# Attention values and the next unit's scores: two runs of small matmuls, or one alternating stream

## The chip, the cores and the metric

The kernel runs on one core of one Trainium2 chip. The metric is the device time of one execution in microseconds (us); a lower time is better. The core has TensorE (PE in the profile, with its weight loads on a row of their own, PEld), VectorE (DVE), ScalarE (ACT), GpSimd (POOL) and SyncE (SP, which issues the transfers).

## The reference

Inputs are q, k and v of shape 8 x 8 x 576 x 64 (batch, heads, sequence, head dimension), and the weights of a gated feed-forward layer.

```python
rel = pos[:, None] - pos[None, :]
mask = (rel >= 0) & (rel < 64)                      # a window of 64 positions
attn = softmax(where(mask, q @ k.T / 8, -1e9))
x = (attn @ v)  # heads side by side: 8 x 576 x 512
h = relu(x @ w_in)                                  # 512 -> 1024
c = conv along the sequence, 3 taps, per channel, zero at the ends
out = (h * sigmoid(c)) @ w_out                      # 1024 -> 512
```

## The kernel before

**Units.** Batch and sequence are laid out in one line of 4608 positions and cut into NU = 12 units of NX = 384. A unit holds NT = 6 blocks of 64 positions. The 8 heads are worked on as NC = 4 groups c (or b) of two heads, so each of the two matmul kinds below comes in four calls a unit.

**Scores** (`qk(u, b)`, line 320). In units 2 to 11 a call multiplies a stationary piece of q, 64 rows (one head's 64 dimensions) by 32 columns (32 positions), with a moving piece of k of 96 positions. The result goes to PSUM partitions `p * 64 + s`, so the columns of the array that a call uses follow from p (0 or 1, the half) and s (0 or 32, the quarter within it); the head h chooses the upper or lower 64 rows of the array and the PSUM tile, `sc[0]` or `sc[1]`. One call is 24 matmuls, which go over eight 64 x 32 pieces of the array. In units 0 and 1 the pieces are 64 x 64 (`wide(u)`), and a call is 12 matmuls.

**Values** (`values(u, c)`, line 437). A call multiplies 128 x 64 stationary pieces of v, using all rows of the array and one half of its columns (head h decides which half), with 64 moving columns of the transposed weights `ub`. One call is 12 matmuls, 6 for each half, h alternating. The result goes to `acc[0]` or `acc[1]`.

All of these are of type f32, and the hardware runs an f32 matmul as two passes: the trace has 24 records for a call of `values` and 48 for a call of `qk` on 64 x 32 pieces.

**The feed-forward part** (`mm1`, line 458, and `mm2`, line 518) is 192 matmuls a unit on the whole 128 x 128 array, 384 or 386 columns each, fp32r with hi and lo parts (three products). Between these matmuls the planner puts the calls of `values` of the next unit and of `qk` of the one after it.

**Who waits for whom.** `row_max` (DVE, line 337) reads `sc` after a call of `qk`, and the next call of `qk` may only write `sc` when it is done. After a call of `values`, `split_hi` (ACT) and `split_lo` (DVE) write `xh` and `xl` of that group, which `mm1` of the unit reads.

**What sets the order.** All work is put into a list by `at(t, engine, cost, ...)`, with a wanted time t, an estimated cost and the tiles that it reads (r) and writes (w). `queued` (line 57) plays the list through with these costs and writes out the order of each engine. It charges 0.12 us when PE goes from one `kind` of matmul to another (`SWITCH`), and where the plan leaves PE idle in the first 110 us it puts in idle matmuls on the tile `spare` (`keep_busy`, line 196). The costs and the 0.12 are numbers of this planner and not measured times. The wanted times of `qk` stand right behind those of `values`, and the key `("turn", c)`, which both write, keeps the calls in turn:

```python
at(t, "PE", 0.70 if wide(u) else 0.62, lambda b=b: qk(u, b), ..., w=bank_keys(u, b) + [("turn", b)],
   kind="tiled" if wide(u) else "eight")                                       # qk, in softmax
at(t, "PE", 0.72, lambda: values(u, c), ..., w=[("acc", ("v", u, c)), ("turn", c)],
   kind="tiled")                                                               # values, in attend
```

Of the kernel before, what the change touches and what calls it, by code (L numbers as in the profile page):

```python
# [15 lines left out]
P = 128  # L16
W = 64
HW = W // 2
KW = W + HW
B, H, S, D = 8, 8, 576, 64  # L20
DM, DFF = H * D, 1024
SB = S // W
NT = 6
NX = NT * W
NU = B * S // NX
# [130 lines left out]
def attention_moe(ctx: ExitStack, tc: tile.TileContext, q, k, v, w_in, conv_w, w_out, out):  # L156
    nc = tc.nc
# [4 lines left out]
    def many(n, shape, dt, name, where=pool):  # L162
        return [where.tile(shape, dt, name=f"{name}{i}") for i in range(n)]

    NB = NT // 2
    ub = many(2, [P, 4, 2 * NT, 32], F32, "ub")
# [7 lines left out]
    qs = pool.tile([P, NC, NX], F32, name="q")  # L174
    ks = pool.tile([P, NC, NX + W], F32, name="k")
    vs = pool.tile([P, NC, NT, 2, D], F32, name="v")
# [14 lines left out]
    acc = many(2, [P, 512], F32, "acc", psum)  # L191
# [15 lines left out]
    def at(t, eng, cost, do, r=(), w=(), kind=None, mb=0):  # L207
        plan.append(Work(t, eng, cost, do, list(r), list(w), kind, mb))
# [76 lines left out]
    def wide(u):  # L285
        return u < BY_PE

    def block(u, b, i):

        first = (u * NT + b % 2 * NB + i) % SB == 0  # L290
        return (P, W if first else 0, 0) if wide(u) else (KW, 0, 2 if first else 1)
# [22 lines left out]
    def banks_of(u, b):  # L314
        return {1: po[2:], 2: po[:2]}.get(b, sc) if u == 0 else sc

    def bank_keys(u, b):
        return {1: [("po", 2), ("po", 3)], 2: [("po", 0), ("po", 1)]}.get(b, [("sc", 0)]) if u == 0 else [("sc", 0)]

    def qk(u, b):  # L320
        g, t0 = b // 2, b % 2 * NB
        rows = W if wide(u) else HW
        for i in range(NB):
            n, o, _ = block(u, b, i)
            for p in range(2):
                for s in range(0, W, rows):
                    r, t = p * W + s, (t0 + i) * W + s
                    for h in range(2):
                        hs = slice(h * D, (h + 1) * D)
                        nc.tensor.matmul(banks_of(u, b)[h][r:r + rows, i * P + o:i * P + n], qs[hs, 2 * g + p, t:t + rows],  # L330
                                         ks[hs, 2 * g + p, t + o:t + n], start=True, stop=True)

    def row_max(u, b):
        for i in range(NB):
            n, o, m = block(u, b, i)
            for h in range(2):
                nc.vector.tensor_tensor_reduce(  # L337
                    out=ss[b][:, i, h, o:n], in0=banks_of(u, b)[h][:, i * P + o:i * P + n], in1=mask[m][:, o:n],
                    scale=-0.125, scalar=3.0e38, op0=ALU.add, op1=ALU.min,
                    accum_out=nms[b][:, 2 * i + h:2 * i + h + 1])  # L340

    def exps(u, b, i):
        n, o, _ = block(u, b, i)
        for h in range(2):
            e = slice(2 * i + h, 2 * i + h + 1)
            x = ss[b][:, i, h, o:n]
            nc.scalar.activation(x, x, AF.Exp, bias=nms[b][:, e], scale=-1.0, accum_out=sms[b][:, e])  # L347

    def guard(b, on):
        on.tensor_scalar_add(sms[b], sms[b], 1e-9)  # L350

    def reciprocal(b):
        nc.vector.reciprocal(rs[b], sms[b])  # L353

    def normalise(u, b, on):
        n = P if wide(u) else KW
        sv = ss[b].rearrange("p t h k -> p (t h) k")[:, :, :n]
        on.tensor_tensor(sv, sv, rs[b].unsqueeze(2).broadcast_to([P, 2 * NB, n]), ALU.mult)  # L358
# [3 lines left out]
    def transpose_pe(b, j):  # L362
        for i in range(NB):
            nc.tensor.transpose(po[b % 2 * 2 + j][:, i * P:(i + 1) * P],
                                ss[b].rearrange("p t h k -> p (t h) k")[:, NB * j + i], ident)

    def untile(b, j):
        o = b % 2 * 2 * NB + NB * j
        nc.scalar.copy(ub[b // 2][:, :, o:o + NB, :].rearrange("p i t q -> p t i q"),  # L369
                       po[b % 2 * 2 + j][:, :NB * P].rearrange("p (t i q) -> p t i q", i=4, q=32))  # L370

    def transpose(b):
        o = b % 2 * 2 * NB
        nc.vector.transpose(
            tbuf[:, b // 2, :3, o:o + 2 * NB, :].rearrange("p j t q -> p t j q"),
            ss[b].rearrange("p t h (j q) -> p (t h) j q", q=HW)[:, :, :3])
# [6 lines left out]
    def place(g, i):  # L383
        for j in range(3):
            o = HW * (i % 2 + j)
            nc.sync.dma_start(ub[g][o:o + HW, i], tbuf[HW * i:HW * (i + 1), g, j])

    def softmax(u, qk_at, ex_at):
        for b in range(4):
            g, t = b // 2, qk_at[b]  # L390
            at(t, "PE", 0.70 if wide(u) else 0.62, lambda b=b: qk(u, b), r=[("q", g, b % 2)] + [("k", g, i) for i in range(b % 2 + 1)], w=bank_keys(u, b) + [("turn", b)],
               kind="tiled" if wide(u) else "eight")
            for i in range(NB):
                if block(u, b, i)[1]:
                    at(t + 0.1, "POOL", 0.2, lambda b=b, i=i: nc.gpsimd.memset(ss[b][:, i, :, :W], 0.0), w=[("s", b, i)])
            at(t + 0.17, "DVE", 1.27 if wide(u) else 1.1, lambda b=b: row_max(u, b),
               r=bank_keys(u, b) + (["mask0"] if wide(u) else ["mask1", "mask2"]), w=[("s", b, i) for i in range(NB)] + [("nm", b)])
            t = ex_at[b]
            for i in range(NB):
                at(t, "ACT", 0.78 if wide(u) else 0.74, lambda b=b, i=i: exps(u, b, i), r=[("nm", b)],  # L400
                   w=[("s", b, i), ("sm", b, i)], kind="exp")
            t += 0.45
            sw = [("sm", b, i) for i in range(NB)]
            if u < 3:
                at(t, "POOL", 0.6, lambda b=b: guard(b, nc.gpsimd), w=sw)
            else:
                at(t, "DVE", 0.15, lambda b=b: guard(b, nc.vector), w=sw)
            at(t, "DVE", 0.15, lambda b=b: reciprocal(b), r=sw, w=[("r", b)])
            if u < 3:
                at(t, "DVE", 1.02 if wide(u) else 0.72, lambda b=b: normalise(u, b, nc.vector), r=[("r", b)], w=[("s", b, i) for i in range(NB)])  # L410
            else:
                at(t, "POOL", 1.15, lambda b=b: normalise(u, b, nc.gpsimd), r=[("r", b)], w=[("s", b, i) for i in range(NB)])
            t += 0.4
            sr = [("s", b, i) for i in range(NB)]
            if u < BY_PE:
                for j in range(2):
                    m = ("po", b % 2 * 2 + j)
                    at(t, "PE", 0.5, lambda b=b, j=j: transpose_pe(b, j), r=sr + ["mask0"], w=[m])
                    at(t + 0.1, "ACT", 0.45, lambda b=b, j=j: untile(b, j), r=[m], w=[("u", g, i) for i in range(4)])
            else:  # L420
                t = max(t, when[-1][2] + 0.1)
                at(t, "DVE", 0.72, lambda b=b: transpose(b), r=sr, w=[("T", g)] + [("bits", i, a) for i in T_BITS[g] for a in range(2)])
                if b % 2:
                    if u == BY_PE:
                        at(t + 0.01, "POOL", 1.0, lambda g=g: zero_blocks(g), w=[("u", g, i) for i in range(4)])
                    for i in range(4):
                        at(t + 0.05, "SP", 2.1, lambda g=g, i=i: place(g, i), r=[("T", g)], w=[("u", g, i)], mb=0.15)

    banks, turn = {}, [0]

    def bank(key):
        if key not in banks:
            banks[key] = turn[0] % 2
            turn[0] += 1
        return banks[key]

    def values(u, c):
        g, p = divmod(c, 2)
        for t in range(NT):
            for h in range(2):  # L440
                nc.tensor.matmul(acc[bank(("v", u, c))][h * D:(h + 1) * D, t * W:(t + 1) * W], vs[:, c, t, h],  # L441
                                 ub[g][:, 2 * p:2 * p + 2, 2 * t + h], start=True, stop=True)

    def split_hi(u, c):
        nc.scalar.copy(xh[u % 2][:, c], acc[bank(("v", u, c))][:, :NX])
# [3 lines left out]

    def attend(u, c, t):  # L450
        g, x = c // 2, u % 2
        at(t, "PE", 0.72, lambda: values(u, c), r=[("v", g)] + [("u", g, i) for i in range(4)], w=[("acc", ("v", u, c)), ("turn", c)],
           kind="tiled")
        at(t + 0.1, "ACT", 0.4, lambda: split_hi(u, c), r=[("acc", ("v", u, c))], w=[("xh", x, c)])
        at(t + 0.2, "DVE", 0.48, lambda: split_lo(u, c), r=[("acc", ("v", u, c)), ("xh", x, c)], w=[("xl", x, c)])

# [149 lines left out]
    kind = None  # L606
    for x in plan:
        if x.eng == "ACT" and x.kind:
            (x.r if x.kind == kind else x.w).append("table")
            kind = x.kind  # L610
# [73 lines left out]
```

## Time and profile before

| | us |
|---|---|
| median of 3 runs (533.0 to 533.41) | 533.32 |
| the profiled execution, time | 533.38 |
| the profiled execution, span from first to last instruction | 531.6 |

| engine | busy us | share of the span |
|---|---|---|
| PE | 523.1 | 98% |
| PE weight loads | 499.2 | 94% |
| ACT | 405.5 | 76% |
| DVE | 381.1 | 72% |
| POOL | 115.9 | 22% |

The granted clock of TensorE is 0.998 over the span. In the rows of the profile a matmul's duration reaches past the start of the next one, since matmuls are pipelined; what a piece of work takes on PE is read from one start to the next. In the names of a row, `acc<-ub,v` is a call of `values`, `sc<-k,q` one of `qk`, `acc<-xh,wih` and the like `mm1`, `po<-gh,woh` and the like `mm2`, and `acc<-spare` an idle matmul. A form such as `64*32 64x96` means a stationary piece of 64 rows and 32 columns and a moving piece of 64 x 96.

### The profile page before, as it was taken

What the parts mean: (1) busy time and instruction counts of PE and PEld (TensorE: products, weight loads), DVE (VectorE), ACT (ScalarE), POOL (GpSimd) and SP (SyncE); (2) the same over time, 40 slices, a digit from 0 to 9 for tenths busy, and PEclk for the clock granted to TensorE, in tenths of its full rate; (3) what the DMA queues carried; (4) which work ended last, traced back from release to release, by engine and by line L of the source; (5) the groups of instructions that cost most, each with busy time, mean ns of one, the idle gap of its engine ahead of it and who ended that gap; (6) DMA issues with size and microseconds to landing.
All of it is one profiled execution on the core that took longest, in us unless ns stands there. A gap on an engine that the chain in (4) does not pass through costs nothing.

```text
span 531.6 us, 14870 instructions
## 1 busy us (share of the span) xinstructions
PE 523.1 (98%) x5802; PEld 499.2 (94%) x5802; DVE 381.1 (72%) x1108; ACT 405.5 (76%) x1034; POOL 115.9 (22%) x208
## 2 busy tenths in 40 slices
PE   9999999999999999999999999999999999999996
PEld 8888889999999999999999999999999999999996
DVE  4899999986677677676686776776776865864552
ACT  5889886799888788689689679779769769653541
POOL 6556663203121121112012022022022011100000
PEclk9999999999999999999999999999999999999999
DMA  8883760166472282273173164254155133110011
GB/s 286 318 300 123 263 224 20 27 181 211 125 249 55 76 252 65 76 236 85 48 241 106 42 222 132 47 198 156 46 185 170 46 121 105 46 61 0 1 60 61
DMA packets 29318, 69.98 MB, mean 132 GB/s; under 512 B 5696, under 2 KB 17472, under 8 KB 29248
## 3 DMA queue, kind: packets, MB, share of 16 engines
q1 hardware_dynamic: 29248, 69.03, 40.5%
q8 instruction: 46, 0.75, 0.6%
q14 instruction: 24, 0.20, 0.1%
HBM read 47.73 MB, written 9.47 MB: 108 GB/s over the span
## 4 chain that ended last, share of the span: by engine, by line
PE 88%; DVE 10%; ACT 1%; issue 1%; POOL 0%
PE po L524 38%; PE acc L461 35%; PE acc L441 6%; PE sc L330 6%; PE acc L201 2%; DVE w L241 1%; DVE c L495 1%; DVE s L337 1%; DVE w L237 1%; DVE wil L255 1%; DVE s L358 1%; DVE w L235 1%; DVE xl L448 1%; ACT ub L369 0%; ACT s L347 0%
## 5 line engine op out<-in xcount | busy, mean ns | idle before, releaser
L524 PE MATMUL po<-gh,woh 128*128 128x386 f32 (+1 forms) x384 | 133.1, 347 | 0.0
L461 PE MATMUL acc<-xh,wih 128*128 128x384 f32 x384 | 131.9, 344 | 1.1 <-DVE xl L448 0.9
L461 PE MATMUL acc<-xh,wil 128*128 128x384 f32 x384 | 129.8, 338 | 0.4 <-DVE wil L255 0.4
L524 PE MATMUL po<-gl,woh 128*128 128x386 f32 (+1 forms) x384 | 130.1, 339 | 0.0
L461 PE MATMUL acc<-xl,wih 128*128 128x384 f32 x384 | 129.7, 338 | 0.0
L524 PE MATMUL po<-gh,wol 128*128 128x386 f32 (+1 forms) x384 | 129.7, 338 | 0.0
L495 DVE SCALAR_TENSOR_TENSOR c<-hbuf,cw,c 128x386 f32<-128x386 f32 (+1 forms) x192 | 110.8, 628 | 19.9 <-ACT c L488 19.0
L347 ACT ACTIVATE s<-s,nm 128x96 f32<-128x96 f32 (+2 forms) x288 | 105.6, 371 | 9.7 <-DVE nm L337 9.3
L358 POOL TENSOR_TENSOR s<-s,r 128x576 f32<-128x576 f32 x36 | 45.7, 1271 | 196.4 <-DVE r L353 196.4
L524 PEld LDWEIGHTS po<-gh,woh 128*128 128x128 f32 x384 | 72.3, 188 | 4.3
L461 PEld LDWEIGHTS acc<-xh,wih 128*128 128x128 f32 x384 | 72.1, 188 | 4.2 <-DVE xl L448 1.6
L461 PEld LDWEIGHTS acc<-xh,wil 128*128 128x128 f32 x384 | 72.2, 188 | 0.7 <-DVE wil L255 0.7
L524 PEld LDWEIGHTS po<-gl,woh 128*128 128x128 f32 x384 | 72.4, 188 | 0.0
L524 PEld LDWEIGHTS po<-gh,wol 128*128 128x128 f32 x384 | 72.4, 188 | 0.0
L461 PEld LDWEIGHTS acc<-xl,wih 128*128 128x128 f32 x384 | 72.1, 188 | 0.0
L337 DVE CUSTOM_DVE_ANT_0 s<-sc,mask 128x96 f32<-128x96 f32 (+2 forms) x276 | 53.2, 254 | 21.3 <-PE sc L330 20.5
L515 DVE TENSOR_TENSOR gl<-c,gh 128x772 fp32r<-128x772 f32 (+1 forms) x48 | 52.8, 1099 | 20.1 <-ACT gh L511 19.5
L502 ACT ACTIVATE c<-c 128x772 f32<-128x772 f32 (+1 forms) x48 | 40.8, 850 | 33.8 <-DVE c L495 33.5
L482 ACT ACTIVATE hbuf<-acc 128x384 f32<-128x384 f32 x64 | 30.6, 487 | 34.7 <-PE acc L461 34.1
L347 ACT ACTIVATION_READ_ACCUMULATOR s<-s,nm 128x1 f32 x288 | 55.1, 191 | 0.0
L488 ACT ACTIVATE c<-hbuf,cw 128x386 f32<-128x386 f32 (+1 forms) x96 | 53.7, 610 | 0.1
L507 DVE TENSOR_TENSOR c<-c,hbuf 128x772 f32<-128x772 f32 (+1 forms) x48 | 45.2, 942 | 9.2 <-ACT c L502 9.2
(64 smaller groups left out, 641.8 us busy)
## 6 DMA issues: line engine op xcount, KB each, us to landing
v<-in_v_dram SPq DMA_DIRECT2D x24, 768.0 KB, 4.7
ub<-T SPq DMA_DIRECT2D x240, 48.0 KB, 2.0
k<-in_k_dram SPq DMA_DIRECT2D x22, 448.0 KB, 5.3
q<-in_q_dram SPq DMA_DIRECT2D x22, 384.0 KB, 6.2
out_dram<-T SPq DMA_DIRECT2D x8, 772.0 KB, 3.5
T<-in_w_in_dram SPq DMA_DIRECT2D x8, 512.0 KB, 5.4
T<-in_w_out_dram SPq DMA_DIRECT2D x8, 512.0 KB, 4.3
out_dram<-T SPq DMA_DIRECT2D x3, 768.0 KB, 6.1
```

Of the source, the lines that this page charges most:

```text
L330: nc.tensor.matmul(banks_of(u, b)[h][r:r + rows, i * P + o:i * P + n], qs[hs, 2 * g + p, t:t + rows], ks[hs, 2 * g + p, t + o:t + n], star ...
L337: nc.vector.tensor_tensor_reduce(out=ss[b][:, i, h, o:n], in0=banks_of(u, b)[h][:, i * P + o:i * P + n], in1=mask[m][:, o:n], scale=-0.125 ...
L347: nc.scalar.activation(x, x, AF.Exp, bias=nms[b][:, e], scale=-1.0, accum_out=sms[b][:, e])
L358: on.tensor_tensor(sv, sv, rs[b].unsqueeze(2).broadcast_to([P, 2 * NB, n]), ALU.mult)
L441: nc.tensor.matmul(acc[bank(("v", u, c))][h * D:(h + 1) * D, t * W:(t + 1) * W], vs[:, c, t, h], ub[g][:, 2 * p:2 * p + 2, 2 * t + h], sta ...
L461: nc.tensor.matmul(acc[bank(("m", u, f))][:, :NX], w[:, f, c], x[u % 2][:, c], start=(c == 0 and j == 0), stop=(c == NC - 1 and j == 2))
L488: nc.scalar.activation(cs[i % 2][:, a, :n], hbuf[:, f, 1:1 + n], AF.Copy, scale=cw[:, 1, f:f + 1])
L495: nc.vector.scalar_tensor_tensor(c, hbuf[:, f, e:e + n], cw[:, e, f:f + 1], c, op0=ALU.mult, op1=ALU.add)
L502: nc.scalar.activation(c, c, AF.Sigmoid)
L507: nc.vector.tensor_tensor(c, c, hbuf[:, 2 * i:2 * i + 2, 1:1 + n], ALU.mult)
L515: nc.vector.tensor_tensor(gls[ring(u, i)][:, :, :n], cs[i % 2][:, :, :n], ghs[ring(u, i)][:, :, :n].bitcast(F32), ALU.subtract)
L524: nc.tensor.matmul(po[o][:, :n], w[:, f, es], x, start=(f == 0 and j == 0), stop=(f == NF - 1 and j == 2))
```

## The change

Calls of `values` for units 1 to 10 and the `qk` call of the unit after them, for the same group, become one call, `both(u, c, c)`. It goes through the 6 blocks for head 0, whose values lie in the first half of the array's columns, and puts two score matmuls of the second half (p = 1) behind each; then through the 6 blocks for head 1 (second half), with two score matmuls of the first half (p = 0) behind each. The planner's cost of it is 1.3, its kind "tiled", and the kind "eight" and the key "turn" are gone. `values` of units 0 and 11, and `qk` of units 0 and 1, stay calls of their own; `qk` there now alternates between the two halves with every matmul. The numbers of wanted times are as they were.

```diff
-    def qk(u, b):
+    def score_steps(u, b):
...
+        def step(i, n, o, p, s, h):
+            r, t, hs = p * W + s, (t0 + i) * W + s, slice(h * D, (h + 1) * D)
+            nc.tensor.matmul(banks_of(u, b)[h][r:r + rows, i * P + o:i * P + n], qs[hs, 2 * g + p, t:t + rows],
+                             ks[hs, 2 * g + p, t + o:t + n], start=True, stop=True)
+
+        return [[lambda i=i, p=p, s=s, h=h: step(i, *block(u, b, i)[:2], p, s, h)
+                 for i in range(NB) for s in range(0, W, rows) for h in range(2)] for p in range(2)]
+
+    def qk(u, b):
+        for x, y in zip(*score_steps(u, b)):
+            x()
+            y()
...
+    def value_steps(u, c):
...
+        return [[lambda t=t, h=h: step(t, h) for t in range(NT)] for h in range(2)]
+
     def values(u, c):
...
+        for x, y in zip(*value_steps(u, c)):
+            x()
+            y()
+
+    def both(u, c, b):
+
+        v, s = value_steps(u, c), score_steps(u + 1, b)
+        for h in range(2):
+            n = len(s[1 - h]) // NT
+            for t, x in enumerate(v[h]):
+                x()
+                for y in s[1 - h][n * t:n * (t + 1)]:
+                    y()
...
+        if u == 0 or u + 1 == NU:
+            at(t, "PE", 0.72, lambda: values(u, c), r=r, w=w, kind="tiled")
+        else:
+            at(t, "PE", 1.3, lambda: both(u, c, c), r=r + needed(c), w=w + bank_keys(u + 1, c), kind="tiled")
```

How this stands in PE's queue is shown at three places, as lists of instructions in order; `x12` is twelve in a row that read alike. In these lists the sizes at a row's end are those of the result, and `sc_108` and `sc_109` are the score tiles of the two heads. First, PE in the middle of the program, the call for group 0 of a unit, before:

```order
L461 MATMUL acc_111<-xl_65,wih 128x384
L441 MATMUL acc_110<-ub_62,v 64x64 x12
L330 MATMUL sc_108<-k,q 32x96
L330 MATMUL sc_109<-k,q 32x96
L330 MATMUL sc_108<-k,q 32x96
```

and PE at such a call after the change:

```order
L553 MATMUL po_115<-gl_102,woh 128x386
L450 MATMUL acc_110<-ub_62,v 64x64
L327 MATMUL sc_108<-k,q 32x96
L327 MATMUL sc_109<-k,q 32x96
L450 MATMUL acc_110<-ub_62,v 64x64
L327 MATMUL sc_108<-k,q 32x96
L327 MATMUL sc_109<-k,q 32x96
```

Twelve `values` matmuls and then 24 of `qk` have become twelve groups of one and two.

Second, PE at the calls for groups 1 and 2, before, where two calls of `values` follow each other, one call of `qk` comes behind them, and the other one 12 matmuls of `mm2` later:

```order
L461 MATMUL acc_110<-xl_65,wih 128x384
L441 MATMUL acc_111<-ub_61,v 64x64 x12
L441 MATMUL acc_110<-ub_62,v 64x64 x12
L330 MATMUL sc_108<-k,q 32x96
L330 MATMUL sc_109<-k,q 32x96
```

and PE at the end of one merged call after the change, where whole-array matmuls follow at once (the next merged call comes 24 of them later here, 12 between groups 1 and 2):

```order
L327 MATMUL sc_109<-k,q 32x96
L450 MATMUL acc_110<-ub_62,v 64x64
L327 MATMUL sc_108<-k,q 32x96
L327 MATMUL sc_109<-k,q 32x96
L490 MATMUL acc_111<-xh_63,wih 128x384
L490 MATMUL acc_111<-xh_63,wil 128x384
```

Each group now has one merged call of its own, so there are four entries from whole-array matmuls a unit, as there were before.

Third, PE in the start, ahead of the first call for unit 1, before:

```order
L364 MATMUL po_112<-ident,s_82 128x128 x3
L364 MATMUL po_113<-ident,s_82 128x128 x3
L441 MATMUL acc_110<-ub_61,v 64x64 x12
L330 MATMUL sc_108<-k,q 32x96
L330 MATMUL sc_109<-k,q 32x96
```

and PE there after the change:

```order
L369 MATMUL po_112<-ident,s_82 128x128 x3
L369 MATMUL po_113<-ident,s_82 128x128 x3
L201 MATMUL sc_108<-spare 128x112 x4
L450 MATMUL acc_110<-ub_61,v 64x64
L327 MATMUL sc_108<-k,q 32x96
L327 MATMUL sc_109<-k,q 32x96
```

Idle matmuls on `spare` stand at other places than before; over the program there are 9 more of them.

More of the change, by code (lines that the diff above doesn't have):

```diff
@@ L318, in bank_keys @@
         return {1: [("po", 2), ("po", 3)], 2: [("po", 0), ("po", 1)]}.get(b, [("sc", 0)]) if u == 0 else [("sc", 0)]
-    def qk(u, b):
+    def score_steps(u, b):
         g, t0 = b // 2, b % 2 * NB
         rows = W if wide(u) else HW
[L323 to L331, printed above, removed]
+        def step(i, n, o, p, s, h):
[8 more added lines that the diff above has]
+            y()
     def row_max(u, b):
@@ L386, in place, with needed @@
             nc.sync.dma_start(ub[g][o:o + HW, i], tbuf[HW * i:HW * (i + 1), g, j])
+    def needed(b):
+        return [("q", b // 2, b % 2)] + [("k", b // 2, i) for i in range(b % 2 + 1)]
     def softmax(u, qk_at, ex_at):
@@ L390, in softmax @@
             g, t = b // 2, qk_at[b]
-            at(t, "PE", 0.70 if wide(u) else 0.62, lambda b=b: qk(u, b), r=[("q", g, b % 2)] + [("k", g, i) for i in range(b % 2 + 1)], w=bank_keys(u, b) + [("turn", b)],
-               kind="tiled" if wide(u) else "eight")
+            if u < 2:
+                at(t, "PE", 0.70, lambda b=b: qk(u, b), r=needed(b), w=bank_keys(u, b), kind="tiled")
             for i in range(NB):
@@ L435, in bank, with step @@
         return banks[key]
-    def values(u, c):
[L438 to L442, printed above, removed]
+    def value_steps(u, c):
+        g, p = divmod(c, 2)
+        def step(t, h):
+            nc.tensor.matmul(acc[bank(("v", u, c))][h * D:(h + 1) * D, t * W:(t + 1) * W], vs[:, c, t, h],
+                             ub[g][:, 2 * p:2 * p + 2, 2 * t + h], start=True, stop=True)
+        return [[lambda t=t, h=h: step(t, h) for t in range(NT)] for h in range(2)]
+    def values(u, c):
+        for x, y in zip(*value_steps(u, c)):
[9 more added lines that the diff above has]
+                    y()
     def split_hi(u, c):
@@ L451, in attend @@
         g, x = c // 2, u % 2
-        at(t, "PE", 0.72, lambda: values(u, c), r=[("v", g)] + [("u", g, i) for i in range(4)], w=[("acc", ("v", u, c)), ("turn", c)],
-           kind="tiled")
+        r, w = [("v", g)] + [("u", g, i) for i in range(4)], [("acc", ("v", u, c))]
+        if u == 0 or u + 1 == NU:
+            at(t, "PE", 0.72, lambda: values(u, c), r=r, w=w, kind="tiled")
+        else:
+            at(t, "PE", 1.3, lambda: both(u, c, c), r=r + needed(c), w=w + bank_keys(u + 1, c), kind="tiled")
         at(t + 0.1, "ACT", 0.4, lambda: split_hi(u, c), r=[("acc", ("v", u, c))], w=[("xh", x, c)])
```

## The prediction

> **What bounds the kernel now.** I read the busy times first, then the chain that ended last, then PE's waits, and then PE's timeline around the calls that the change merges.
>
> ```profile
> PE 523.1 (98%) x5802; PEld 499.2 (94%) x5802; DVE 381.1 (72%) x1108; ACT 405.5 (76%) x1034; POOL 115.9 (22%) x208
> PE 88%; DVE 10%; ACT 1%; issue 1%; POOL 0%
> PE acc L441 <- DVE xl L448: 1.1, 1, 1.1
> PE acc L461 <- DVE xl L448: 0.9, 2, 0.5
> 65.00:110.00 45.00, 44.31 (x500) 42.22 (x501) 44.77 (x104) 35.01 (x87) 17.23 (x21) 1.00 0.33 108
> 110.00:450.00 340.00, 340.00 (x4039) 324.89 (x4038) 238.37 (x762) 280.96 (x728) 55.82 (x101) 1.00 0.43 134
> ```
>
> The first line is the busy time of each engine, the second the chain by engine, the next two are PE's longest waits (total, times, longest), and the last two are stretches of the span with the busy time of PE, PEld, DVE, ACT and POOL, the granted clock (1.00), and DMA. From 110 to 450 us PE is busy without a gap, at full clock, while DVE has 102 us to spare and ACT 59. So PE's own queue sets the time, and whatever a merged call takes longer or shorter on PE passes to the end one for one. Only before 110 us, where DVE is nearly as full as PE, could some be hidden or lost.
>
> **What the merged calls take today.** These rows are PE's timeline: start, duration, what, how many records.
>
> ```profile
> 253.38 0.33 PE L524 MATMUL po<-gl,woh 128*128 128x386 f32 x1
> 253.64 0.92 PE L441 MATMUL acc<-ub,v 128*64 128x64 f32 x24
> 254.49 0.83 PE L330 MATMUL sc<-k,q 64*32 64x96 f32 x48
> 255.25 0.44 PE L461 MATMUL acc<-xh,wih 128*128 128x384 f32 x1
> 255.53 0.33 PE L461 MATMUL acc<-xh,wil 128*128 128x384 f32 x1
> ...
> 266.01 1.62 PE L441 MATMUL acc<-ub,v 128*64 128x64 f32 x48
> 267.55 0.83 PE L330 MATMUL sc<-k,q 64*32 64x96 f32 x48
> 268.32 0.45 PE L524 MATMUL po<-gh,woh 128*128 128x384 f32 x1
> ...
> 270.62 0.83 PE L330 MATMUL sc<-k,q 64*32 64x96 f32 x48
> 271.39 0.44 PE L524 MATMUL po<-gh,woh 128*128 128x384 f32 x1
> ```
>
> From the first start to the start of the next whole-array matmul, one call of values and one of scores take 255.25 - 253.64 = 1.61 us (0.85 to the first score, 0.76 from there). Two calls of values and one of scores take 268.32 - 266.01 = 2.31, one of scores alone 271.39 - 270.62 = 0.77. The first of these calls starts at 45.18 and the last at 437.84:
>
> ```profile
> 45.18 0.92 PE L441 MATMUL acc<-ub,v 128*64 128x64 f32 x24
> 437.84 0.92 PE L441 MATMUL acc<-ub,v 128*64 128x64 f32 x24
> ```
>
> Between them the timeline has 22 of the first kind, 9 of the second and 9 of the third (four of the first for unit 1, then two, one and one a unit): 22 x 1.61 + 9 x 2.31 + 9 x 0.77 = 63.1 us for the 40 calls of each that the change merges. The cost of entering from the whole array (253.38 to 253.64) is paid four times a unit before and after, so it drops out.
>
> **The price of a change of piece.** A call of values uses pieces of 128 rows x 64 columns, a call of scores 64 x 32. After the change the two alternate twelve times in a call. These rows take the passages apart; the first two and the fourth are short windows, so that their counts stop at a known record.
>
> ```profile
> 253.64 0.33 PE L441 MATMUL acc<-ub,v 128*64 128x64 f32 x3
> 254.33 0.23 PE L441 MATMUL acc<-ub,v 128*64 128x64 f32 x2
> 254.34 0.22 PE L441 MATMUL acc<-ub,v 128*64 128x64 f32 x1
> 254.49 0.35 PE L330 MATMUL sc<-k,q 64*32 64x96 f32 x9
> 255.08 0.24 PE L330 MATMUL sc<-k,q 64*32 64x96 f32 x1
> ...
> 458.77 0.22 PE L441 MATMUL acc<-ub,v 128*64 128x64 f32 x1
> 458.92 0.44 PE L461 MATMUL acc<-xh,wih 128*128 128x384 f32 x1
> ```
>
> Two passes of values start together, one in each half, and the third record starts at 253.64 + 0.33 - 0.22 = 253.75: a second pass in the same half comes 0.11 us after the first when the call has just begun. The last pass of values starts at 254.34 and the first score at 254.49, 0.15 later. At 458.77, where whole-array matmuls follow, the gap is the same 0.15. Later in a run a pair of value passes comes every 0.06 us (24 records more lengthen the 0.85 to 267.55 - 266.01 = 1.54), so some 0.1 of the 0.15 is waiting. Eight scores start on eight pieces; the ninth record, the second pass of the first piece, starts at 254.49 + 0.35 - 0.24 = 254.60, 0.11 after the first. From the last score to the whole array it is 255.25 - 255.08 = 0.17.
>
> So a change from values to scores costs as much as one to the whole array, though the first scores lie in the first half (p = 0 comes first) and the last value matmul in the second. If only the columns in use had to run empty, that score could have started after the pass at 254.33, at 254.48. That is 0.01 earlier and at the edge of what these rows resolve; it speaks for a wait of the whole array at a change of piece, but the trace has no place where two shapes meet in separate columns only. The price of that has to be bounded from both sides.
>
> The Trainium skill, page "TensorEngine Tiling (Array Packing)", section "Key Properties", says: "Changing tiling mode (not just tile) drains the TensorE". The trace's two gaps of 0.15 agree, and by that rule this change pays 24 drains a call.
>
> **The sum.** I take the wait of the whole array at each change of piece, since the one passage from values to scores in the trace behaves so.
>
> - One group of the new stream: value matmul, 0.11 to its second pass and 0.15 to the first score; two scores on two pieces, 0.01 between them, 0.11 to their second passes, 0.17 to the next value matmul: 0.26 + 0.29 = 0.55 us.
> - One merged call: 12 x 0.55 = 6.60 us, in place of 1.58 on average. 40 calls: 264.0 - 63.1 = +200.9 us.
> - Ends of this term: if second passes came at their running distance (0.06 and 0.08, the latter below), a group is 0.47, a call 5.64 and the term +162.5. If each wait were a further 0.015 longer (the spread between 0.15 and 0.17), a group is 0.58, a call 6.96 and the term +215.3.
> - Nine more idle matmuls in the start: 34 passes take 15.13 - 11.24 = 3.89 us, so one of two passes 0.23, nine 2.0 us. They stand where the plan leaves PE idle; I take half, +1.0, ends 0 and +2.0.
>
> ```profile
> 11.24 4.05 PE L201 MATMUL acc<-spare 128*128 128x112 f32 x34
> 15.13 0.27 PE L364 MATMUL po<-ident,s 128*128 128x128 f32 x1
> ```
>
> - The `qk` calls of units 0 and 1 in another order: same pieces, same count, 0. Their cover is the start, in which idle matmuls stand between the calls.
> ```profile
> 254.81 0.46 ACT L445 CAST xh<-acc 128x384 fp32r<-128x384 f32 x1
> 256.42 0.55 DVE L448 TENSOR_TENSOR xl<-acc,xh 128x384 fp32r<-128x384 f32 x1
> ```
>
> - The values of group 2 come 12 `mm2` matmuls later, about 2.1 us; `mm1` of that unit begins only 24 whole-array matmuls (4.2 us) behind the merged call of group 3, while the two splits were done 256.42 + 0.55 - 254.49 = 2.5 us after the end of the values here: 0. Without that cover PE would wait for `split_lo` as it does twice above, 0.5 at the longest. `row_max` and both splits stay behind the call's end as before, and DVE and ACT have room; if PE is longer, they wait more and set nothing. No DMA is added, and none is moved past another in SP's queue by more than the calls themselves move.
>
> Together +201.9 on the profiled execution's 533.4: 735 us. The median shown is 533.32, the same to 0.1. Alone, this case reaches from 533.4 + 162.5 = 696 to 533.4 + 215.3 + 2.0 = 751.
>
> **The rivals.**
>
> *Only the columns in use have to run empty* (faster). Then in each half values and scores simply follow one another, and the halves run side by side. The value run takes its 0.85 in either half. The scores have six passes on each of four pieces, as they had on each of eight. The 17th record, third pass of the first piece, starts at 254.49 + 0.43 - 0.24 = 254.68, 0.08 behind the ninth:
>
> ```profile
> 254.49 0.43 PE L330 MATMUL sc<-k,q 64*32 64x96 f32 x17
> ```
>
> Six passes then need 0.11 + 4 x 0.08 + 0.02 + 0.17 = 0.62 in place of 0.76; today's last records come late, and a stream spread over a longer time need not have that. A call is 1.47, 40 of them 58.8, the term -4.3 and the time 530.1. If the two exits of a call also hid behind the other half (0.08 a call), it would be 527; 526 without the idle matmuls. For it: pieces of one shape plainly run side by side. Against it: the 0.15 to a score in the other half. The same section of that page of the Trainium skill says that tiles operate independently; this trace shows it for one shape (eight scores within 0.05), and no run here for two.
>
> *Nothing to measure.* As above, but the second phase's values, behind the first phase's scores in the queue, start some 0.1 late: 1.57 a call, 62.8, -0.3 and the time 534.1.
>
> *The exchange of halves waits for both* (mildly slower). Two shapes run side by side, but both halves must be empty in the middle: two value runs of 0.85 one after the other, 1.70 a call, 68.0, +4.9 and 539.3.
>
> **How the numbers follow.** 0.58 for the wait at each change (735). The rest is for the three cases in which shapes do run together, since a trace with no such meeting can't exclude them: 0.22 for 530, 0.10 for 534, 0.10 for 539. A measurement of this kernel tells about 0.2% (1 us) from no change, so: faster 0.22, same 0.10, slower 0.68. To leave out no more than 0.2 the range has to hold both groups: 526 to 751. The likeliest case's own range is 696 to 751.
>
> **What will show it.** In the changed kernel's timeline, a merged call from its first value to the next whole-array matmul: about 6.6 us if I am right, 1.47 to 1.70 if shapes run together. Inside it, the first score starts 0.15 or more behind a value's last pass if the array empties; if scores start within 0.02 of a value matmul in the other half, my step on the price of a change of piece is wrong, and with it the whole 201 us. Whole-array matmuls should keep their pitch, and PE's waits for other engines should stay near zero.

## The result: 733 us, slower by 37%

The changed kernel takes 733.23 us (median of 4 runs, 732.01 to 734.89) where the kernel before takes 533.37 (533.0 to 534.49): 1.374 times as long, 95% interval 1.3705 to 1.3784. The forecast was 735, in a range of 526 to 751.

The page of the changed kernel (busy times, chain by engine and by line, granted clock in 40 slices), its longest wait of PE, and two groups of instructions:

```profile
PE 722.3 (99%) x5820; PEld 604.5 (83%) x5820; DVE 380.5 (52%) x1108; ACT 409.6 (56%) x1034; POOL 113.7 (16%) x208
PE 95%; DVE 2%; ACT 1%; DMA 1%; POOL 0%; SPq 0%; issue 0%
PE acc L490 28%; PE po L553 28%; PE sc L327 19%; PE acc L450 17%; PE po L201 1%; PE acc L201 1%; DMA q<-in_q_dram 1%; DVE s L342 0%; DVE w L241 0%; DVE s L363 0%; PE po L369 0%; DVE c L524 0%; PE sc L201 0%; DVE w L237 0%; PE po L327 0%; ACT ub L374 0%
PEclk9999999999999999999999999999999999999999
...
PE acc L490 <- ACT hbuf L507: 1.6, 1, 1.6
...
L490 PE MATMUL acc<-xl,wih 128*128 128x384 f32 x384 | 129.8, 338 | 0.0
L342 DVE CUSTOM_DVE_ANT_0 s<-sc,mask 128x96 f32<-128x96 f32 (+2 forms) x276 | 53.5, 256 | 212.5 <-PE sc L327 206.9
```

DVE, ACT and POOL work as long as before, within 5 us each. PE's row is fuller than before, 99%, though it does the same matmuls and 9 idle ones more: a pair of value passes lasts 0.33 us in the rows below and the next row starts 0.26 after it, so the busy time also covers the wait at a change. The tell-tale figures are PEld, which fell from 94% to 83%, and the chain by line, where scores and values went from 12% of 532 us to 36% of 730. The whole-array matmuls cost what they cost before (338 ns a row, clock full). DVE's `row_max` now spends 207 us waiting for scores, and that costs nothing.

PE's timeline at a merged call, its beginning and its end:

```profile
310.25 0.34 PE L490 MATMUL acc<-xl,wih 128*128 128x384 f32 x1
310.52 0.33 PE L450 MATMUL acc<-ub,v 128*64 128x64 f32 x2
310.78 0.35 PE L327 MATMUL sc<-k,q 64*32 64x96 f32 x4
311.06 0.33 PE L450 MATMUL acc<-ub,v 128*64 128x64 f32 x2
311.32 0.27 PE L327 MATMUL sc<-k,q 64*32 64x96 f32 x2
...
316.50 0.33 PE L450 MATMUL acc<-ub,v 128*64 128x64 f32 x2
316.76 0.35 PE L327 MATMUL sc<-k,q 64*32 64x96 f32 x4
317.05 0.45 PE L553 MATMUL po<-gh,woh 128*128 128x386 f32 x1
```

The rows no longer merge into one of 24 and one of 48: each group of a value matmul (two passes) and two scores (four) stands by itself, and from the last start of one kind to the first of the other there are 0.15 us (310.52 + 0.33 - 0.22 = 310.63 to 310.78) or 0.17. Values to scores is 310.78 - 310.52 = 0.26 us, scores to values 311.06 - 310.78 = 0.28, a group 0.54. A call is 317.05 - 310.52 = 6.53, and all 40 calls are alike: 261.2 us together, in place of 63.1. That is +198.1 of the span's +198.8 (730.4 less 531.6).

The weight loads at the first of these changes, in a short window:

```profile
310.57 0.14 PEld L450 LDWEIGHTS acc<-ub,v 128*64 128x64 f32 x1
310.78 0.11 PEld L327 LDWEIGHTS sc<-k,q 64*32 64x32 f32 x2
```

The weights of the second value pass are loaded from 310.57, 0.06 ahead of that pass at 310.63. Those of the first score are not loaded ahead: their load starts at 310.78, when the score itself starts. So the 0.15 us lies before the load and is not the time of a load. "The array runs empty" is this document's name for that wait; the ends of the rows don't show it (the values' row ends at 310.85, after the first score has started), but the starts show that nothing of the new shape begins until the wait is over.

### The profile page after: what moved, and what is told of

It is laid out like the page before. It is cut to its first block, busy times and chain, and to the rows that moved or that the text cites. A ratio compares the mean times of both kernels' runs of the same rounds, so it can differ in the third digit from the quotient of the medians.

```text
span 730.4 us, 14927 instructions
## 1 busy us (share of the span) xinstructions
PE 722.3 (99%) x5820; PEld 604.5 (83%) x5820; DVE 380.5 (52%) x1108; ACT 409.6 (56%) x1034; POOL 113.7 (16%) x208
## 4 chain that ended last, share of the span: by engine, by line
PE 95%; DVE 2%; ACT 1%; DMA 1%; POOL 0%; SPq 0%; issue 0%
PE acc L490 28%; PE po L553 28%; PE sc L327 19%; PE acc L450 17%; PE po L201 1%; PE acc L201 1%; DMA q<-in_q_dram 1%; DVE s L342 0%; DVE w L241 0%; DVE s L363 0%; PE po L369 0%; DVE c L524 0%; PE sc L201 0%; DVE w L237 0%; PE po L327 0%; ACT ub L374 0%
## 5 line engine op out<-in xcount | busy, mean ns | idle before, releaser
L327 PE MATMUL sc<-k,q 64*32 64x96 f32 (+2 forms) x2064 | 176.1, 256 | 0.0
L450 PE MATMUL acc<-ub,v 128*64 128x64 f32 x1152 | 164.9, 243 | 0.6 <-DMA v<-in_v_dram 0.6
L450 PEld LDWEIGHTS acc<-ub,v 128*64 128x64 f32 x1152 | 97.8, 135 | 75.4 <-issue 6.2
L490 PE MATMUL acc<-xh,wih 128*128 128x384 f32 x384 | 133.6, 348 | 2.2 <-ACT hbuf L507 1.6
L553 PE MATMUL po<-gh,woh 128*128 128x386 f32 (+1 forms) x384 | 131.3, 342 | 0.1
L471 ACT CAST xh<-acc 128x384 fp32r<-128x384 f32 x48 | 22.9, 481 | 192.5 <-PE acc L450 192.5
L327 PEld LDWEIGHTS sc<-k,q 64*32 64x32 f32 (+1 forms) x2064 | 71.5, 106 | 33.2 <-DVE nm L342 0.2
```

The source lines that it names most:

```text
L490: nc.tensor.matmul(acc[bank(("m", u, f))][:, :NX], w[:, f, c], x[u % 2][:, c], start=(c == 0 and j == 0), stop=(c == NC - 1 and j == 2))
L553: nc.tensor.matmul(po[o][:, :n], w[:, f, es], x, start=(f == 0 and j == 0), stop=(f == NF - 1 and j == 2))
```

## The experiments

The theory: at each change from one shape of piece (its rows x columns) to another the whole array runs empty, whatever columns or rows are in use. Its rivals: that the new plan carries the loss; that it belongs to using one half at a time; that columns in use matter; that alternating kinds, halves or PSUM tiles costs by itself; that only rows, or only columns, of the shape count. Times are medians; ratios are against the kernel before on the same chip.

**How many changes.** Three kernels keep the merged call in the plan and differ from the changed one only inside it. First, one passage:

```diff
-        v, s = value_steps(u, c), score_steps(u + 1, b)
-        for h in range(2):
...
+        values(u, c)
+        qk(u + 1, b)
```

> The merged call is kept in the plan (its cost, its place, the idle matmuls), but inside it all 12 value matmuls come first and then all 24 scores: one passage from values to scores in a call, in place of 23 changes. Theory (the whole array runs empty at each change of piece): a call takes 0.85 + 0.76 = 1.61 us as the single calls did before, 40 of them 64.4 in place of 63.1, and the rest of the changed plan costs the +0.7 that the trace of the changed kernel leaves outside the merged calls: 535.4 us. Rival (the new plan, its order and its idle matmuls, carry the loss): near 733.

Then k value matmuls in a row and the 2k scores of the other half behind them, k = 6 and k = 2 (the kernels have the number where k stands here):

```diff
-            for t, x in enumerate(v[h]):
-                x()
-                for y in s[1 - h][n * t:n * (t + 1)]:
-                    y()
+            for t in range(0, NT, k):
+                for x in v[h][t:t + k]:
+                    x()
+                for y in s[1 - h][n * t:n * (t + k)]:
+                    y()
```

> Same matmuls, same halves, but the six value matmuls of a half in a row and then the twelve scores of the other half: 3 changes inside a call, in place of 23. Theory (each change costs the same wait): value run 0.84, score run on four pieces 0.63, twice: 2.94 us a call, 117.6 for 40, so 533.4 + 117.6 - 63.1 + 0.7 = 589. Rival (the loss belongs to using one half at a time, not to the number of changes): the call stays near 6.5 and the time near 733. Rival (only columns in use run empty): value run and scores of the other half side by side, 1.5 to 1.7 a call, 531 to 539.

> Two value matmuls and then four scores, six groups a call: 11 changes inside a call. Theory: values 0.11 + 2 x 0.06 + 0.15 = 0.38, scores 0.02 + 0.11 + 0.17 = 0.30, so 0.68 a group, 4.05 a call and 533.4 + 162 - 63.1 + 0.7 = 633. Rival (loss not by the number of changes): 733.

| value matmuls in a row | changes inside a call | a call, us | expected, us | time, us | ratio (95%) |
|---|---|---|---|---|---|
| 12 | 1 | 1.61 | 535.4 | 540.85 | 1.0135 (1.011 to 1.016) |
| 6 | 3 | 2.94 | 589 | 591.34 | 1.107 (1.104 to 1.111) |
| 2 | 11 | 4.05 | 633 | 634.04 | 1.187 (1.184 to 1.191) |
| 1 (the change) | 23 | 6.53 | | 733.23 | 1.374 (1.3705 to 1.3784) |

PE's timeline for six in a row:

```profile
160.15 0.91 PE L450 MATMUL acc<-ub,v 128*64 128x64 f32 x12
160.99 0.70 PE L327 MATMUL sc<-k,q 64*32 64x96 f32 x24
161.62 0.91 PE L450 MATMUL acc<-ub,v 128*64 128x64 f32 x12
162.46 0.70 PE L327 MATMUL sc<-k,q 64*32 64x96 f32 x24
163.09 0.45 PE L554 MATMUL po<-gh,woh 128*128 128x384 f32 x1
```

The time goes with the number of changes. From 11 to 23 of them a call grows by 2.48, 0.41 for every two. Worked out from the forecast's rows, 0.18 of that is the array's emptying (the gaps of 0.15 and 0.17, less the running distances 0.06 and 0.08); 0.08 is the start of the two runs, whose second passes come 0.11 behind the first and not 0.06 and 0.08; and 0.15 is that two scores use two pieces, while four scores on four pieces take no longer. The step from 1 to 3 is larger, 1.33, since there the second half of the array falls idle as well: in the rows above, 12 value passes take 0.84 in one half, and the 24 of both halves took 0.85 before. The other half's scores don't start until 160.99. So two shapes do not run side by side even when a run of one lies wholly in columns that the other doesn't use. The rivals of the plan (near 733 in the first row) and of one half at a time (near 733 in the second) have fallen; what the first row has over its forecast is taken up below.

**Whether the columns matter.** The scores go to the same half as the values beside them:

```diff
-            n = len(s[1 - h]) // NT
+            n = len(s[h]) // NT
...
-                for y in s[1 - h][n * t:n * (t + 1)]:
+                for y in s[h][n * t:n * (t + 1)]:
```

> The same alternation with the scores in the same half of the columns as the values beside them, so that each change meets columns in use. Theory (the whole array runs empty whatever the columns): no difference, 733 us, 6.53 a call. Rival (separate columns spare at least a part of the wait, loading of weights or running empty): longer, by up to the 0.05 that a hidden weight load is worth at each of 24 changes, 1.2 a call and 48 us in all: up to 781.

733.07 us, ratio 1.3725 (1.3697 to 1.3753), 6.53 a call. The same rows as in the changed kernel, to 0.01:

```profile
190.02 0.33 PE L450 MATMUL acc<-ub,v 128*64 128x64 f32 x2
190.28 0.36 PE L327 MATMUL sc<-k,q 64*32 64x96 f32 x4
190.56 0.33 PE L450 MATMUL acc<-ub,v 128*64 128x64 f32 x2
```

Which half the scores use makes no difference that these runs show.

**Whether it is the shape, and which side of it.** The kernels of this part compute other scores than the reference: on 128 rows they are sums over two heads, and on 64 x 64 pieces half of the rows see keys 32 positions too early. They are run for their times alone. In the first one the scores have the shape of the values, 128 x 64:

```diff
-        rows = W if wide(u) else HW
+        rows = W
...
-            r, t, hs = p * W + s, (t0 + i) * W + s, slice(h * D, (h + 1) * D)
+            r, t, hs = p * W + s, (t0 + i) * W + s, slice(h * D, (h + 1) * D) if wide(u) else slice(0, P)
```

> Scores on the value matmuls' own shape: 128 rows x 64 columns, one in place of each pair, so a stream of twelve times one value and one score matmul that alternates halves as the change does but never changes shape. (It contracts over both heads' rows, so its scores are sums over two heads.) Theory (the change of shape costs): no wait inside; each half works through 12 value passes of 0.058 and 12 score passes of 0.083, 1.7 us, and 0.2 at the ends: 1.85 to 2.2 a call, 545 to 559 us. Rival (alternating between kinds, banks or halves costs, whatever the shape): 0.26 + 0.27 a group, 6.4 a call, 727.

556.36 us, ratio 1.042 (1.037 to 1.047), 2.02 a call. PE's timeline, some rows from early in a call, from its middle and from its end:

```profile
194.82 0.22 PE L450 MATMUL acc<-ub,v 128*64 128x64 f32 x1
194.85 0.25 PE L327 MATMUL sc<-k,q 128*64 128x96 f32 x1
194.88 0.22 PE L450 MATMUL acc<-ub,v 128*64 128x64 f32 x1
194.93 0.25 PE L327 MATMUL sc<-k,q 128*64 128x96 f32 x1
...
195.43 0.55 PE L327 MATMUL sc<-k,q 128*64 128x96 f32 x6
195.76 0.28 PE L450 MATMUL acc<-ub,v 128*64 128x64 f32 x2
...
196.73 0.45 PE L553 MATMUL po<-gh,woh 128*128 128x386 f32 x1
```

Here both kinds do run side by side: a score pass starts 0.03 behind a value pass, in the other half, and neither waits for the other to end. Where the halves exchange roles (195.43 to 195.76) the scores of the first phase run out, and the array is not emptied for the values that follow. Kinds, halves and PSUM tiles alternate as in the changed kernel, so none of these is the cost. What is new is the shape, with one score matmul in place of two behind each value matmul. This is also roughly what the change would have looked like if its idea had held.

Then only one side of the shape differs. Scores of 64 x 64 (rows alone):

```diff
-        rows = W if wide(u) else HW
+        rows = W
```

> Scores on 64 x 64 pieces, one in place of each pair (the second 32 rows of each then see keys 32 positions too early): only the rows of the piece differ from the value matmuls' 128 x 64. Theory: any change of shape runs the array empty: 0.26 + 0.28 a group, 6.5 a call, 730 us. Rival (only a different number of columns does): no wait, value passes set the pace, 1.4 to 1.6 a call, 525 to 535.

863.80 us, ratio 1.6175 (1.6113 to 1.6238), far above both. The columns of the first view are start, end, length, then busy time and count of PE, PEld, DVE, ACT and POOL, then the granted clock:

```profile
222.60:231.30 8.70, 8.70 (x49) 5.61 (x48) 0.27 (x2) 1.86 (x4) 0.94 (x1) 0.71 0.15 59
310.00:321.00 11.00, 11.00 (x50) 6.90 (x49) 0.27 (x2) 0.75 (x2) 0.00 (x0) 0.50 0.10 41
...
222.62 0.33 PE L450 MATMUL acc<-ub,v 128*64 128x64 f32 x2
222.87 0.38 PE L327 MATMUL sc<-k,q 64*64 64x96 f32 x2
223.18 0.33 PE L450 MATMUL acc<-ub,v 128*64 128x64 f32 x2
```

At the beginning of a call a group takes 223.18 - 222.62 = 0.56, the forecast for a wait at each change (0.54); then the granted clock falls to half, and a whole call at half clock takes 10.96. The run answers the question only in these first rows, so it was made again with each score matmul issued twice:

```diff
+            w = rows if wide(u) else W
+            if not wide(u):
+                r, t = p * W, (t0 + i) * W
-            nc.tensor.matmul(banks_of(u, b)[h][r:r + rows, i * P + o:i * P + n], qs[hs, 2 * g + p, t:t + rows],
+            nc.tensor.matmul(banks_of(u, b)[h][r:r + w, i * P + o:i * P + n], qs[hs, 2 * g + p, t:t + w],
```

> As the run in which only the rows of the piece differ (64 x 64 scores between 128 x 64 values), with each score matmul issued twice, so that two score matmuls stand behind each value matmul as in the change, one on the upper and one on the lower 64 rows. That run ran at a granted clock of 0.83, which hides the price of a change. Theory (a change of rows alone makes the array run empty; the clock fell since too little of the array was at work): clock 1.0, values 0.26 and scores 0.31 a group, 6.8 a call, 744 us. Rival (the low clock comes with this pair of shapes): clock again near 0.83 and over 850. Rival (rows alone are free, the low clock made the calls long): under 560 at full clock.

745.64 us, ratio 1.395 (1.392 to 1.399), 6.85 a call, granted clock 1.0:

```profile
192.74 0.33 PE L453 MATMUL acc<-ub,v 128*64 128x64 f32 x2
193.00 0.38 PE L330 MATMUL sc<-k,q 64*64 64x96 f32 x4
193.31 0.33 PE L453 MATMUL acc<-ub,v 128*64 128x64 f32 x2
```

A change of rows alone empties the array. Now columns alone, 128 x 32:

```diff
-            r, t, hs = p * W + s, (t0 + i) * W + s, slice(h * D, (h + 1) * D)
+            r, t, hs = p * W + s, (t0 + i) * W + s, slice(h * D, (h + 1) * D) if wide(u) else slice(0, P)
```

> Scores on 128 x 32 pieces, two behind each value matmul as in the change (contracted over both heads): only the columns of the piece differ. Theory: any change of shape runs the array empty: 6.5 a call, 733 us. Rival (only a different number of rows does): no wait; the scores' 12 passes of 0.083 on each of two pieces set the pace, 1.85 to 2.2 a call, 545 to 559.

810.50 us, ratio 1.518 (1.513 to 1.522), 8.47 a call, again above both:

```profile
206.53 0.33 PE L450 MATMUL acc<-ub,v 128*64 128x64 f32 x2
206.79 0.52 PE L327 MATMUL sc<-k,q 128*32 128x96 f32 x4
207.24 0.33 PE L450 MATMUL acc<-ub,v 128*64 128x64 f32 x2
```

Values to scores is 0.26 as elsewhere, but scores to values 0.45 in place of 0.28. The mistake was in the experiment's forecast: on 128 rows the head no longer chooses a piece, so the two scores behind a value matmul lay on the same 32 columns and their passes came one after another. With the order changed so that they lie on two pieces:

```diff
-                 for i in range(NB) for s in range(0, W, rows) for h in range(2)] for p in range(2)]
+                 for i in range(NB) for h in range(2) for s in range(0, W, rows)] for p in range(2)]
```

> As the run in which only the columns of the piece differ (128 x 32 scores between 128 x 64 values), with the order of the scores changed so that the two behind a value matmul lie on two different 32-column pieces; before, both lay on the same piece and their four passes came one after another (0.08 apart, 8.47 a call). Theory (a change of columns alone makes the array run empty, and the extra length was those two passes): 0.26 + 0.29 a group, 6.55 a call, 733 us. Rival (128 x 32 pieces cost more at each change): it stays near 8.5 a call and 810.

734.07 us, ratio 1.374 (1.370 to 1.378), 6.57 a call:

```profile
173.57 0.33 PE L450 MATMUL acc<-ub,v 128*64 128x64 f32 x2
173.83 0.36 PE L327 MATMUL sc<-k,q 128*32 128x96 f32 x4
174.12 0.33 PE L450 MATMUL acc<-ub,v 128*64 128x64 f32 x2
```

A change of columns alone empties it too. Rows, columns or both: from the last value pass to the first score it is 0.15 us in all three, and from the last score pass to the next value 0.17 to 0.18.

**What the plan costs.** With one passage in a call, 540.85 us stood where 535.4 was expected. Its trace shows the calls at 1.61, except the first, and PE waiting there:

```profile
44.70 0.57 PE L450 MATMUL acc<-ub,v 128*64 128x64 f32 x12
45.64 0.45 PE L450 MATMUL acc<-ub,v 128*64 128x64 f32 x6 [0.37 <-ACT ub L374]
47.07 0.45 PE L450 MATMUL acc<-ub,v 128*64 128x64 f32 x6 [0.98 <-ACT ub L374]
47.45 1.20 PE L327 MATMUL sc<-k,q 64*32 64x96 f32 x48
48.58 0.77 PE L201 MATMUL po<-spare 128*128 128x112 f32 x2
```

The first guess was the planner's cost of a merged call (one passage is kept inside it):

```diff
-            at(t, "PE", 1.3, lambda: both(u, c, c), r=r + needed(c), w=w + bank_keys(u + 1, c), kind="tiled")
+            at(t, "PE", 1.6, lambda: both(u, c, c), r=r + needed(c), w=w + bank_keys(u + 1, c), kind="tiled")
```

> As the run with one passage in a call, with the planner's cost of a merged call set from 1.3 to 1.6, near the 1.61 that it was measured to take. That run came out 5.5 us above its forecast, with calls of 1.61 as expected and PE waits in the first 110 us that the changed kernel does not have. Theory A (the plan's too low cost put PE's work of the start ahead of what DVE and ACT deliver): the waits go, 535 to 537 us. Theory B (one merged call for each group in the start is itself the cause, whatever its cost in the plan): 539 to 542.

542.76 us, ratio 1.016 (1.014 to 1.0175): theory A has fallen, and the time lies slightly above the range of theory B too. A truer cost made the plan put in six more idle matmuls, and it was no faster; why not stays open. The second guess (again with one passage) left the calls of unit 1 single, with the wanted times, the key and the kinds that they had:

```diff
-            if u < 2:
-                at(t, "PE", 0.70, lambda b=b: qk(u, b), r=needed(b), w=bank_keys(u, b), kind="tiled")
+            if u < 3:
+                at(t, "PE", 0.70 if wide(u) else 0.62, lambda b=b: qk(u, b), r=needed(b), w=bank_keys(u, b) + [("turn", b)],
+                   kind="tiled" if wide(u) else "eight")
...
-        if u == 0 or u + 1 == NU:
-            at(t, "PE", 0.72, lambda: values(u, c), r=r, w=w, kind="tiled")
+        if u < 2 or u + 1 == NU:
+            at(t, "PE", 0.72, lambda: values(u, c), r=r, w=w + [("turn", c)], kind="tiled")
```

> As the run with one passage in a call, but the calls of unit 1, which lie in the start, are left as single calls with the order that they had before, so the start up to about 110 us has the instructions of the kernel before. Theory (5.5 us of that run's loss lie in the start, where the merged calls move the idle matmuls and what waits for DVE and ACT): the start is as before, and only the 0.15 us a unit remains that four calls of 1.61 take over 1.61, 2.31, 0.77 and 1.61: nine units, 1.4, so 534.8 to 535 us. Rival (merging into one call a group costs all along the steady part, by later values and splits): 539 to 541.

534.51 us, ratio 1.0013 (0.9998 to 1.0028). So some 6 us of the plan's loss lie in the start, and in the steady part one merged call a group costs about what the single calls cost. What in the start makes up the 6 is known in part. The first call is 2.3 us longer (3.88 in place of 1.61): its two waits are 1.35 of that, and its scores take 1.13 (47.45 to 48.58) in place of 0.76, since the granted clock fell to half in this execution. There are 9 idle matmuls more, 2.0 by the 0.23 each of the forecast. And PE's longest wait in this run is a later one, 2.7 us for `hbuf` from 108 us on, which the kernel before does not have:

```profile
47.50:50.90 3.40, 3.40 (x60) 3.12 (x60) 3.40 (x5) 3.17 (x5) 1.29 (x2) 0.51 0.03 5
PE acc L485 <- ACT hbuf L502: 2.7, 1, 2.7
```

These three come to 7.0, more than the 6 to be explained, so they probably overlap in part with waits that the kernel before has as well. In the changed kernel the waits for `ub` are gone, probably because its calls are four times as long and leave DVE and ACT the time; of the wait for `hbuf`, 1.6 is left.

No kernel here beats the one before; in none of them were the two kinds both of their own shape and side by side.

## Why the prediction was right

- **PE's queue sets the time.** Right. +198.1 us in the merged calls came out as +198.8 of span.
- **The price of a change of piece.** Right, and it was the step on which all hung, given 0.58. The two gaps of 0.15 in the kernel before, one to a score in the other half and one to the whole array, were its sign in the trace; the pass in the other half only 0.01 earlier was the weak point, and the run with scores in the same half settles it: columns do not count. The rule of the Trainium skill named in the prediction (page "TensorEngine Tiling (Array Packing)", section "Key Properties") is borne out, and these runs give it a price: about 0.09 us beyond the running distance at each change, and 0.03 to 0.05 for the first passes of a run.
- **The group, 0.55.** It is 0.54: rounding of rows to 0.01 gave the 2.8 us by which 264.0 exceeds 261.2.
- **Nine more idle matmuls, +1.0.** What lies outside the calls is +0.7. That the number fits is in part luck: half of the nine was a choice between 0 and 2.0 with no row behind it, the same start costs some 6 us where calls are short, and the term left out the waits of the start altogether, which long calls hide for the most part. Had the calls been free, the rivals' 530 to 539 would probably have been too low by such waits.
- **Values of group 2 later, at no cost.** Right in the steady part; PE has one wait of 1.6 us, for `hbuf`, at 130 us, which the prediction didn't name. The waits that it lists as the longest before leave out one of 1.0 us, the first idle matmuls' for `spare`; nothing hangs on it, since it is there before and after.
- **The range.** 526 to 751 was wide enough for this case and all its rivals, so the time inside it says little; what counts is that it fell in the likeliest case's own 696 to 751, and that the call (6.53 for 6.6) and the 0.15 before the first score came out as forecast.
- **The rivals.** Columns emptied alone, and both exchange variants, are ruled out for two shapes. What they describe does happen for one shape (2.02 a call with scores on 128 x 64).

## What to carry to other kernels

In these runs two kinds of small f32 matmul shared the array only where their pieces had the same rows and the same columns (128 x 64 beside 64 x 32, 64 x 64 and 128 x 32 did not). So count the changes of shape, give each what the gap in a trace says (0.15 and 0.17 us here, so that one value matmul took 0.26 up to the first score and two scores 0.28 up to the next value), and put each shape into as few runs as its buffers allow. The price can be read off a trace that has only one such passage: the gap from the last start of one kind to the first of the other, less the running distance. And a changed plan can cost time elsewhere (some 6 us in the start here, which a truer planner's cost didn't mend), so price the plan apart from the step (one passage in the merged call did it here).

## What the hardware showed that was not expected

With one 64 x 64 score matmul behind each value matmul the granted clock fell to 0.50 over whole calls, and to 0.83 over the run. As long as the clock was full, no pause between two starts inside a call was longer than the 0.17 us of the changed kernel, which kept its clock at 0.54 us a group. Each score issued twice, at 0.57 a group, brought the clock back to 1.0. So pauses alone don't decide this clock. Two scores on 64 x 32, as in the changed kernel, cover the same part of the array as one on 64 x 64, so the covered area does not explain it either. What does differ is the number of passes in a group, four where the clock fell and six where it held; whether that is what counts, and where the limit lies, these runs don't say.

Matmuls on different pieces of one shape do not keep to the order of the program. In the stream of one shape the first phase has six scores, 12 passes. By 195.76, when the first value pass of the second phase starts, 14 score passes have started: two of the second phase have gone past the value matmul that stands ahead of them in the queue. The count is 14 in 39 of the 40 calls and 13 in the other.
